# Attention issued one group less ahead of the feed-forward, its output transposed by DMA from tile 3 on, and values loaded group by group

## The chip, the cores and the metric

The kernel runs on one core of one Trainium2 chip. The metric is device time in microseconds. A core has TensorE (PE; its weight loads are PEld), VectorE (DVE), ScalarE (ACT), GpSimd (POOL) and SyncE (SP), on whose queue (SPq) all DMA issues stand. The traces list each engine's instructions as a stream of its own, and show DVE and SP keeping to program order even where a later instruction could go.

## The reference, cut to what matters

```python
# attention: batch 8, heads 8, sequence 576, head size 64, causal window of 64
scores = np.where(mask, (q @ k.T) / 8, -1e9)       # mask: 0 <= i - j < 64
x = softmax(scores) @ v                            # then to 4608 tokens x 512
# feed-forward, width 1536
g = x @ w_gate
out = (g * sigmoid(g) * (x @ w_val)) @ w_out
```

Inputs and output are float32; the kernel computes in bfloat16 with float32 sums.

## The kernel before

The 4608 tokens are 36 groups of 128. Four groups are one token tile of 512 for the feed-forward; two groups are one k/q tile of 256. For a group, attention is `scores` (16 small matmuls, exp on ACT, a product with the mask on DVE), `products` (16 small matmuls, a reciprocal and a product on DVE that give `x_b`) and a transpose of `x_b` into `xT`, which the feed-forward reads. `step(t, m)` is one feed-forward step: 4 gate and 4 value matmuls, tanh on ACT, then two DVE instructions (`sg`, `hT`) that `finish` the step before. `project` is 12 matmuls and the output write.

```python
ps_a = ctx.enter_context(tc.tile_pool(name="ps_a", bufs=3, space=PSUM))   # attention
ps_f = ctx.enter_context(tc.tile_pool(name="ps_f", bufs=2, space=PSUM))   # gate, value: 2 each

def turn1(n, nm):               # k or q, by DMA: two transposes on SP's queue
    x_b = words.pop((nm, n))
    for i in range(2):
        ...
        sp.dma_start_transpose(out=ring[:, :, o:o + P], in_=x_b[:, i])

def turn2(n, nm, eng): ...      # k or q, on PE: eight transposes and a copy on `eng`

def turn_x(g):                  # x_b -> xT on PE: four transposes and a copy on ACT
    ...
    for p in range(4):
        nc.tensor.transpose(tp[:, p, :], x_b[:, P * p:P * p + P], identb[:])
    act.copy(xT[t][:, :, off:off + P], tp[:])

def step(t, m, c0=0, n=512):
    st = gv(t, m, c0, n)        # matmuls, tanh
    if pend: finish(pend)       # sg and hT of the step BEFORE this one
    pend = st
...
for w in range(8, NG):          # one round: three steps, one group of attention, one projection
    t, s = divmod(w, 4)
    n, odd = w // 2, w % 2
    step(t, 3 * s)
    if w + 6 < NG: scores(w + 6)
    if w + 4 < NG: turn_x(w + 4)
    ...                          # casts of k and q on POOL
    step(t, 3 * s + 1)
    if w + 5 < NG: products(w + 5, (0,))
    if w + 6 < NG: cast_v(w + 6, pool)
    step(t, 3 * s + 2)
    if w + 5 < NG: products(w + 5, (1,))
    ...                          # turn1 of k or q
    project(t - 1, s)
    ...                          # loads
```

Ahead of the loop the same pieces are written out by hand, with half-width steps (`A`, `B`) and full ones (`F`). There k and q of tiles 0 to 3 are transposed on PE, of tiles 4 and later by DMA.

The softmax here doesn't subtract the row's maximum and nothing guards it: scores larger than these inputs give would overflow.

## Time and profile before

| | before |
|---|---|
| time, median of 2 | 371.24 us |
| span of the profiled run | 370.2 us |
| PE busy | 93% |
| first two waits of PE | DVE `sg` 4.8 us, DMA `qT` 4.6 us |
| usual round of the loop | 9.01 us |

The page: busy time, then rows of tenths over 40 slices of the span.

```profile
PE 345.2 (93%) x2750; PEld 181.5 (49%) x2797; DVE 231.1 (62%) x503; ACT 154.0 (42%) x276; POOL 113.5 (31%) x159
PE   8787998989779999999999999999999999999995
PEclk9999999999899999999999999999999999999999
```

PE is nearly full from slice 13 on. The two 7s in slices 11 and 12 (about 93 to 111 us) are a dip. The waits of PE (what for; us in total, times, longest) name it:

```profile
PE g_ps L237 <- DVE sg L248: 4.8, 10, 0.8
PE s_ps L161 <- DMA qT<-q_fb: 4.6, 2, 2.6
```

The windows view (columns: stretch, its length, busy time of PE, PEld, DVE, ACT and POOL, granted PE clock, DMA share, GB/s) shows a lower granted clock in the dip too, and just behind it (0.83, 0.96 and 0.87):

```profile
90.00:100.00 10.00, 7.33 (x65) 4.16 (x65) 3.47 (x10) 2.88 (x7) 4.71 (x7) 0.83 0.90 175
100.00:110.00 10.00, 7.59 (x79) 4.06 (x79) 4.41 (x12) 4.09 (x9) 2.13 (x2) 0.96 0.81 185
110.00:120.00 10.00, 9.89 (x70) 4.77 (x71) 5.37 (x12) 3.35 (x7) 3.86 (x5) 0.87 0.97 192
```

The clock record of this trace has two stretches of 3.41 us at half clock here, from 95.56 and from 109.22 us (windows view of 95.56:98.97 and of 109.22:112.63: 0.50 each); most of the second lies in the third window.

One usual round, from the timeline (start, duration, engine, line, operation). It began at 199.92 us; these lines, a selection, run from the tanh of its first step to the first matmul of its third:

```profile
201.03 0.60 ACT L242 ACTIVATE th<-g_ps 128x512 f32<-128x512 f32 x1 [0.32 <-PE g_ps L237]
201.74 0.41 PE L161 MATMUL s_ps<-qT,kT 64*128 64x64 bf16 x16
202.09 0.40 PE L205 MATMUL xtp<-identb,x_b 128*128 128x128 bf16 x4
202.19 1.08 ACT L167 ACTIVATE E<-s_ps 128x512 bf16<-128x512 f32 x2 [0.55 <-PE s_ps L161]
202.81 0.91 DVE L168 TENSOR_TENSOR E<-E,mask 128x512 bf16<-128x512 bf16 x2 [2.84 <-ACT E L167]
203.65 0.68 DVE L248 SCALAR_TENSOR_TENSOR sg<-th,g_ps 128x512 f32<-128x512 f32 x1
204.38 1.02 PE L237 MATMUL g_ps<-xT,wg 128*128 128x512 bf16 x4
```

The third step reuses the gate's PSUM buffer of the first, and `sg` is what frees it. Note also why `sg` comes so late: this `sg` belongs to the first step, and its inputs were ready when `th` ended at 201.63. DVE then stood idle until 202.81 (2.84 us in all), because the mask products of the scores come before `sg` in its program order.

### The profile page before, as it was taken

The page shows a single profiled execution, that of the slowest core. Times are in us where ns is not written, and L with a number is a line of the kernel's source. Part 1 is how long each engine was busy: PE and PEld are TensorE (multiplying, and loading weights), DVE is VectorE, ACT ScalarE, POOL GpSimd, SP SyncE. Part 2 cuts the span into 40 slices and gives each one's busy share as a digit, 9 for nine tenths or more (in the row PEclk, how much of TensorE's full clock was granted, in tenths as well). Part 3 has the DMA queues.
Part 4 walks back from the last instruction along what each step waited for, and adds up shares of the span by engine and source line. Part 5 has one row for each costly group of instructions (what it writes and reads, how often), then busy time and mean ns, then how long its engine had stood idle before and what let it go on. Part 6 is the DMA issues. An engine that isn't in the chain of part 4 may idle for free.

```text
span 370.2 us, 7165 instructions
## 1 busy us (share of the span) xinstructions
PE 345.2 (93%) x2750; PEld 181.5 (49%) x2797; DVE 231.1 (62%) x503; ACT 154.0 (42%) x276; POOL 113.5 (31%) x159
## 2 busy tenths in 40 slices
PE   8787998989779999999999999999999999999995
PEld 3456556546334444444444545444444445444442
DVE  5577798697245666666666666666666666644520
ACT  3554755444243443444344444444444443323311
POOL 2554585463314350605060606060605120000000
PEclk9999999999899999999999999999999999999999
DMA  8999999899889965857688869675744300001112
GB/s 204 322 252 266 290 313 241 150 159 188 176 186 186 197 149 119 175 124 158 132 172 120 177 123 149 147 168 126 143 96 104 87 28 30 28 30 41 44 58 85
DMA packets 147841, 54.99 MB, mean 149 GB/s; under 512 B 127328, under 2 KB 141664, under 8 KB 147808
## 3 DMA queue, kind: packets, MB, share of 16 engines
q1 hardware_dynamic: 147808, 54.54, 66.6%
q8 instruction: 22, 0.36, 0.5%
q14 instruction: 11, 0.09, 0.1%
HBM read 37.75 MB, written 9.44 MB: 127 GB/s over the span
## 4 chain that ended last, share of the span: by engine, by line
PE 74%; DVE 6%; DMA 6%; SPq 5%; ACT 5%; issue 2%; POOL 2%; ACTq 0%; POOLq 0%
PE o_ps L254 24%; PE g_ps L237 21%; PE v_ps L237 19%; DMA q_f<-in_q_dram 4%; SPq L93 4%; DVE E L168 3%; PE s_ps L161 3%; PE w_ps L266 2%; ACT E L167 2%; PE xtp L205 2%; PE ao_ps L183 2%; PE ao_ps L187 2%; DMA qT<-q_fb 1%; DVE sg L248 1%; SPq L123 1%
## 5 line engine op out<-in xcount | busy, mean ns | idle before, releaser
L237 PE MATMUL g_ps<-xT,wg 128*128 128x512 bf16 (+1 forms) x457 | 111.9, 358 | 6.9 <-DVE sg L248 4.8
L237 PE MATMUL v_ps<-xT,wv 128*128 128x512 bf16 (+1 forms) x472 | 112.3, 360 | 0.9 <-ACT wv L103 0.5
L254 PE MATMUL o_ps<-wo,hT 128*128 128x512 bf16 x419 | 98.4, 384 | 0.7
L242 ACT ACTIVATE th<-g_ps 128x512 f32<-128x512 f32 (+1 forms) x120 | 67.3, 561 | 71.0 <-PE g_ps L237 66.9
L248 DVE SCALAR_TENSOR_TENSOR sg<-th,g_ps 128x512 f32<-128x512 f32 (+1 forms) x120 | 75.1, 626 | 20.9 <-ACT th L242 20.9
L168 DVE TENSOR_TENSOR E<-E,mask 128x512 bf16<-128x512 bf16 x72 | 36.9, 526 | 74.8 <-ACT E L167 73.4
L249 DVE TENSOR_TENSOR hT<-sg,v_ps 128x512 bf16<-128x512 f32 (+1 forms) x120 | 76.1, 634 | 8.4
L237 PEld LDWEIGHTS <-wv 128*128 128x128 bf16 x480 | 47.0, 98 | 48.3 <-issue 1.4
L237 PEld LDWEIGHTS <-wg 128*128 128x128 bf16 x480 | 44.8, 98 | 41.7 <-issue 7.0
L254 PEld LDWEIGHTS <-hT 128*128 128x128 bf16 x432 | 40.8, 99 | 46.1 <-issue 2.2
L105 POOL CAST q_fb<-q_f 128x1024 bf16<-128x1024 f32 x17 | 17.9, 1053 | 114.6 <-DMA q_f<-in_q_dram 112.4
L167 ACT ACTIVATE E<-s_ps 128x512 bf16<-128x512 f32 x72 | 39.1, 596 | 20.1 <-PE s_ps L161 20.1
L105 POOL CAST ve<-v_f 64x512 bf16<-64x512 f32 x71 | 44.3, 624 | 4.4
L192 DVE TENSOR_TENSOR x_b<-ao_ps,r 128x256 bf16<-128x256 f32 x72 | 30.5, 424 | 2.5
L105 POOL CAST vo<-v_f 128x512 bf16<-128x512 f32 x36 | 22.3, 621 | 25.8 <-DMA v_f<-in_v_dram 14.2
L105 POOL CAST k_fb<-k_f 128x1024 bf16<-128x1024 f32 x17 | 18.1, 1063 | 38.1 <-DMA k_f<-in_k_dram 32.6
L183 PE MATMUL ao_ps<-ve,E 128*128 128x65 bf16 x288 | 26.6, 194 | 2.2 <-DVE x_b L192 1.2
L183 PEld LDWEIGHTS <-E 128*128 128x128 bf16 x288 | 22.0, 98 | 9.6 <-DVE E L168 1.5
L187 PE MATMUL ao_ps<-vo,E 128*128 128x65 bf16 x288 | 26.6, 194 | 0.0
L206 ACT COPY xT<-xtp 128x512 bf16<-128x512 bf16 x36 | 21.2, 590 | 12.1 <-PE xtp L205 12.1
L187 PEld LDWEIGHTS <-E 128*128 128x128 bf16 x288 | 20.1, 98 | 6.5 <-issue 0.3
L161 PE MATMUL s_ps<-qT,kT 64*128 64x64 bf16 x576 | 14.9, 191 | 7.3 <-DMA qT<-q_fb 4.6
(73 smaller groups left out, 136.3 us busy)
## 6 DMA issues: line engine op xcount, KB each, us to landing
v_f<-in_v_dram SPq DMA_DIRECT2D x32, 256.0 KB, 4.8
k_f<-in_k_dram SPq DMA_DIRECT2D x25, 256.0 KB, 3.9
q_f<-in_q_dram SPq DMA_DIRECT2D x25, 256.0 KB, 4.2
w_f<-in_moe_w_gate_dram SPq DMA_DIRECT2D x6, 512.0 KB, 7.6
w_f<-in_moe_w_val_dram SPq DMA_DIRECT2D x6, 512.0 KB, 6.5
wo_f<-in_moe_w_out_dram SPq DMA_DIRECT2D x6, 512.0 KB, 6.5
k_f<-in_k_dram SPq DMA_DIRECT2D x3, 512.0 KB, 6.9
q_f<-in_q_dram SPq DMA_DIRECT2D x3, 512.0 KB, 8.1
```

Of the source, the lines that this page charges most:

```text
L105: eng.tensor_copy(y, x)
L161: nc.tensor.matmul(ps[a][:, p, 1 - b], kT[g // 2 % KR][y, p, o:o + P], qT[g // 2 % QR][y, p, o:o + 64], tile_position=(64 * a, 0),)
L167: act.activation(e, ps[a][:], AF.Exp, scale=0.125)
L168: dve.tensor_mul(e, e, mk[:].unsqueeze(1).to_broadcast([P, 4, 2, 64]))
L183: nc.tensor.matmul(o_ps[:, i, :], E[:, e + P:e + 2 * P], ve[g % VR][:, y, :], start=True, stop=False,)
L187: nc.tensor.matmul(o_ps[:, i, :], E[:, e:e + P], vo[g % VR][:, y, :], start=False, stop=True,)
L192: dve.tensor_mul(x_b[:, 256 * h:256 * h + 256].rearrange("r (y d) -> r y d", y=4), o_ps[:, :, 0:D], r[:].unsqueeze(2).to_broadcast([P, 4, D]),
L237: nc.tensor.matmul(ps[:, 0:n], w[:, c, P * m:P * m + P], xT[t][:, c, c0:c0 + n], start=(c == 0), stop=(c == 3),)
L242: act.activation(th[:, 0:n], g_ps[:, 0:n], AF.Tanh, scale=0.5)
L248: dve.scalar_tensor_tensor(sg[:, 0:n], th[:, 0:n], 1.0, g_ps[:, 0:n], ALU.add, ALU.mult)
L249: dve.tensor_mul(hT[t][:, m, c0:c0 + n], sg[:, 0:n], v_ps[:, 0:n])
L254: nc.tensor.matmul(o_ps[:], hT[t][:, c, P * s:P * s + P], wo[:, c, :], start=(c == 0), stop=(c == 11),)
```

## The change

Its intent is to take work off PE (transposes by DMA), to ask for k, q and v later (a shorter lead), and to spread the loads. The core of the diff:

```diff
+    def load_vg(g): ...            # values of one group, not of two
+    def turn_x1(g):                # x_b -> xT by DMA
+        t, off = g // 4, P * (g % 4)
+        if off == 0:
+            xT[t] = xpool.tile([P, 4, 512], BF16, name="xT", tag="xT")
+        sp.dma_start_transpose(out=xT[t][:, :, off:off + P], in_=xb.pop(g)[:])
 # ahead of the loop: tiles 4 and 5 of k and q, and the order of all pieces (cut)
-    load1(4, k, "k_f")
-    load1(4, q, "q_f")
+    load(4, k, "k_f")              # 512-byte runs
+    load(4, q, "q_f")
-    turn1(4, "k_f")
-    turn1(4, "q_f")
+    turn2(4, "k_f", dve)           # on PE; tile 5 likewise
+    turn2(4, "q_f", act)
-    products(12)                   # and scores(13), cast_v(13), cast and turn of tiles 7 q, 8 k
     ...
     for w in range(8, NG):
         step(t, 3 * s)
-        if w + 6 < NG:
-            scores(w + 6)
         if w + 4 < NG:
-            turn_x(w + 4)
+            products(w + 4)
         ...
         step(t, 3 * s + 1)
         if w + 5 < NG:
-            products(w + 5, (0,))
+            scores(w + 5)
+        if w + 4 < NG:
+            turn_x1(w + 4)
         step(t, 3 * s + 2)
-        if w + 5 < NG:
-            products(w + 5, (1,))
         ...
         project(t - 1, s)
         ...
-        if odd and n + 4 < NB:
-            load_v(n + 4)
+        if w + 7 < NG:
+            load_vg(w + 7)
```

More of the change, by code (lines that the diff above doesn't have):

```diff
@@ L97, in load_v, with load_vg @@
         load1(n, v, "v_f")
+    def load_vg(g):
+        if g % 2 == 0:
+            staged["v_f", g // 2] = stage.tile([P, 2, H, D], FP32, name="v_f", tag="v_f")[:]
+        x_f = staged["v_f", g // 2]
+        for r, m, b, s, t in segments(P * g, P, 1):
+            sp.dma_start(x_f[r:r + m, g % 2], v[b, :, s:s + t, :].rearrange("h r d -> r h d"))
     words = {}
@@ L413 @@
     turn_x(5)
-    load1(4, k, "k_f")
-    load1(4, q, "q_f")
+    load(4, k, "k_f")
+    load(4, q, "q_f")
     load_v(4)
+    cast_k(3, "k_f", pool)
     F(0, 10)
-    cast_k(3, "k_f", pool)
     cast_k(3, "q_f", pool)
+    keys_before(3)
+    turn2(3, "k_f", dve)
+    F(0, 11)
+    turn2(3, "q_f", act)
     cast_v(6, pool)
     cast_v(7, pool)
-    F(0, 11)
-    keys_before(3)
-    turn2(3, "k_f", dve)
     A(1, 0)
-    turn2(3, "q_f", act)
+    for s in range(2):
+        casts_o(s, pool)
     A(1, 1)
-    for s in range(3):
-        casts_o(s, pool)
-    A(1, 2)
-    scores(6)
-    A(1, 3)
-    scores(7)
-    products(6)
-    for s in range(3, 6):
-        casts_o(s, pool)
-    A(1, 4)
-    turn_x(6)
-    products(7)
+    scores(6)
+    A(1, 2)
+    scores(7)
+    A(1, 3)
+    products(6)
+    A(1, 4)
+    products(7)
+    turn_x(6)
+    for s in range(2, 4):
+        casts_o(s, pool)
     A(1, 5)
@@ L443 @@
     cast_k(4, "q_f", pool)
-    turn1(4, "k_f")
-    turn1(4, "q_f")
-    keys_before(4)
-    load1(5, k, "k_f")
-    load1(5, q, "q_f")
-    load_v(5)
-    B(1, 0)
-    F(1, 6)
+    load(5, k, "k_f")
+    load(5, q, "q_f")
+    load_v(5)
+    A(1, 6)
+    B(1, 0)
+    for s in range(4, 6):
+        casts_o(s, pool)
+    B(1, 1)
+    F(1, 7)
+    keys_before(4)
+    turn2(4, "k_f", dve)
     cast_v(8, pool)
     cast_v(9, pool)
-    F(1, 7)
+    F(1, 8)
+    turn2(4, "q_f", act)
+    F(1, 9)
     scores(8)
-    F(1, 8)
+    project(0, 0)
+    B(1, 2)
+    scores(9)
     products(8)
-    F(1, 9)
-    turn_x(8)
-    scores(9)
     cast_k(5, "k_f", pool)
     cast_k(5, "q_f", pool)
-    turn1(5, "k_f")
-    turn1(5, "q_f")
-    keys_before(5)
     load1(6, k, "k_f")
@@ L469 @@
     F(1, 10)
+    turn_x(8)
     products(9)
@@ L474 @@
     turn_x(9)
-    scores(10)
-    project(0, 0)
-    B(1, 1)
-    products(10)
-    B(1, 2)
+    keys_before(5)
+    turn2(5, "k_f", dve)
+    project(0, 1)
+    B(1, 3)
+    turn2(5, "q_f", act)
     cast_k(6, "k_f", pool)
+    turn1(6, "k_f")
+    keys_before(6)
     cast_k(6, "q_f", pool)
-    turn1(6, "k_f")
     turn1(6, "q_f")
-    keys_before(6)
     load1(7, k, "k_f")
     load1(7, q, "q_f")
-    load_v(7)
+    load_vg(14)
+    B(1, 4)
+    scores(10)
+    project(0, 2)
+    products(10)
+    B(1, 5)
+    scores(11)
     turn_x(10)
-    scores(11)
-    project(0, 1)
-    B(1, 3)
+    B(1, 6)
     products(11)
     cast_v(12, pool)
-    B(1, 4)
-    turn_x(11)
-    scores(12)
-    project(0, 2)
-    B(1, 5)
-    products(12)
-    cast_v(13, pool)
     cast_k(7, "k_f", pool)
@@ L503 @@
     keys_before(7)
-    cast_k(7, "q_f", pool)
-    turn1(7, "q_f")
+    scores(12)
     load1(8, k, "k_f")
-    load1(8, q, "q_f")
-    scores(13)
     project(0, 3)
-    cast_k(8, "k_f", pool)
-    turn1(8, "k_f")
-    keys_before(8)
-    load1(9, k, "k_f")
+    turn_x(11)
     for w in range(8, NG):
@@ L519 @@
         step(t, 3 * s)
-        if w + 6 < NG:
-            scores(w + 6)
         if w + 4 < NG:
-            turn_x(w + 4)
-        if odd and n + 5 < NB:
-            cast_k(n + 5, "k_f", pool)
-        if not odd and n + 4 < NB:
-            cast_k(n + 4, "q_f", pool)
+            products(w + 4)
+        if odd and n + 4 < NB:
+            cast_k(n + 4, "k_f", pool)
+        if not odd and n + 3 < NB:
+            cast_k(n + 3, "q_f", pool)
+        if w + 5 < NG:
+            cast_v(w + 5, pool)
         step(t, 3 * s + 1)
         if w + 5 < NG:
-            products(w + 5, (0,))
-        if w + 6 < NG:
-            cast_v(w + 6, pool)
+            scores(w + 5)
+        if w + 4 < NG:
+            turn_x1(w + 4)
         step(t, 3 * s + 2)
-        if w + 5 < NG:
-            products(w + 5, (1,))
-        if odd and n + 5 < NB:
-            turn1(n + 5, "k_f")
-            keys_before(n + 5)
-        if not odd and n + 4 < NB:
-            turn1(n + 4, "q_f")
+        if odd and n + 4 < NB:
+            turn1(n + 4, "k_f")
+            keys_before(n + 4)
+        if not odd and n + 3 < NB:
+            turn1(n + 3, "q_f")
         project(t - 1, s)
         if odd and n + 5 < NB:
-            load1(n + 5, q, "q_f")
-        if odd and n + 4 < NB:
-            load_v(n + 4)
-        if not odd and n + 6 < NB:
-            load1(n + 6, k, "k_f")
+            load1(n + 5, k, "k_f")
+        if w + 7 < NG:
+            load_vg(w + 7)
+        if not odd and n + 4 < NB:
+            load1(n + 4, q, "q_f")
     flush()
```

## The prediction

> **What bounds the kernel now.** TensorE. The page gives PE 345.2 of 370.2 us (93%), and the chain of waits lies on PE for 74%. In the steady loop (w = 8 to 35, from 117 us on) the windows view shows PE busy 9.3 to 9.95 of every 10 us; one round w takes 9.02 us (timeline: rounds start at 199.92, 208.93, 217.96 us). The other loss is early: the windows 90-100 and 100-110 us have PE busy 7.3 and 7.6. The waits view names it: scores wait twice for the DMA transposes of q (4.6 us in total, 2.56 us at 92 us and 2.00 us at 106 us) (1.25 us to issue, 2.5 to 3.5 us to land, in one in-order SP queue). After each of the two waits the granted clock falls (0.83 and 0.87 in those windows): the 12 matmuls of the projection at 95.1 us take 4.29 us instead of 2.60, and about the same 1.7 us is lost from 108.8 us on. [...] So each wait costs about 4 us, the two about 8 us.
>
> **Removed.** 24 of 36 PE transposes of the attention output (groups 12 to 35), each 0.24 us of PE stream (201.74 scores, 202.08 transposes, 202.32 next step): 5.7 us, all on the critical engine. DMA transposes of k and q of tiles 4 and 5 (8 issues) leave the early queue, and their loads get 512-byte runs; so the early waits for DMA should go: up to 8 us.
>
> **Added.** 32 PE transposes (k, q of tiles 4, 5): 8 take 0.44 us, so 1.8 us, plus copies of 1.0 to 1.2 us on DVE and ACT. In the loop one DMA transpose per round: SP issue grows from about 5.5 to 6.8 us per 8.8 us round; DMA share from about 0.77 to an estimated 0.87 (512 more packets beside some 4,200).
>
> **Moved.** Attention runs one group less ahead. Values loaded per group even the queue out (3 loads each round, not 4 and 2).
>
> **New risk.** The last transpose of a token tile must land before the next tile's first step. By my reading x_b is ready about 4 us into the round, behind this round's three loads; issue 1.2 us, landing 3.5 to 5 us after issue start: 7.5 to 9 us, with the deadline near 8.7. Six such hand-overs (tiles 3 to 8) at 0 to 1 us each: I allow 1.5 us. q's lead falls to one round, about 2.5 us of slack. The early half-width steps are DVE-bound as before (0.83 us DVE against 0.87 PE, plus attention work); I allow 1.5 us for new early waits.
>
> **Sum.** 371.2 - 8.0 - 5.7 + 1.8 + 1.5 + 1.5 = 362.3. I predict 362 us, 80% range 357 to 368. Faster by over 2% (under 363.8): 0.65; within 2%: 0.31; slower: 0.04.
>
> **Would show it right.** Round period near 8.78 us; no wait of scores for qT by DMA, and granted clock 1.0 from 85 to 125 us; 48 transposes of x_b on PE; the loop starts near 110 us, not 117; DMA share in the loop up by about 0.1.
>
> **Would show it wrong.** First-step matmuls waiting for xT by DMA over 1 us per tile, with the clock falling after them; scores waiting for qT in odd rounds; load landing times growing past 6 us; new PE waits for DVE or POOL between 55 and 110 us.

The sum is 362.3 us, and its 8.0 us are the two waits (2.56 and 2.00 us) and about 1.7 us of slower matmuls behind each (4.29 us for 2.60 behind the first).

## The result

| | before | after |
|---|---|---|
| time, median of 2 | 371.24 us | 356.16 us |
| span of the profiled run | 370.2 us | 354.1 us |
| usual round | 9.01 us | 8.70 us |

The ratio is 0.9594 (95% interval 0.9553 to 0.9635). A ratio here and below is the mean time of one kernel's fast runs over that of the other's of the same rounds, so not quite the ratio of the medians quoted. The change is faster by about 15 us; 9 were predicted, and the time is 0.8 us under the predicted range.

The page after:

```profile
PE 335.0 (95%) x2696; PEld 175.6 (50%) x2741; DVE 233.4 (66%) x507; ACT 144.0 (41%) x255; POOL 113.1 (32%) x159
PE   7697999999889999999999999999999999999995
PEclk9999999999999999999999999999999999999999
```

The waits of PE, its first and the largest of scores for `qT`. No wait for a DMA of `qT` is left; that one is for a PE transpose's copy:

```profile
PE g_ps L252 <- DVE sg L263: 2.1, 4, 0.8
PE s_ps L169 <- ACT qT L111: 0.9, 2, 0.7
```

The same two windows; the clock is whole:

```profile
90.00:100.00 10.00, 8.09 (x105) 5.19 (x104) 6.24 (x19) 4.93 (x10) 1.27 (x2) 1.00 1.10 158
100.00:110.00 10.00, 9.83 (x73) 4.79 (x74) 5.82 (x12) 3.60 (x8) 5.74 (x8) 1.00 0.98 174
```

A usual round, begun at 187.11 us, from its scores to the first matmul of the next round:

```profile
191.15 0.41 PE L169 MATMUL s_ps<-qT,kT 64*128 64x64 bf16 x16
191.59 1.08 ACT L175 ACTIVATE E<-s_ps 128x512 bf16<-128x512 f32 x2 [0.55 <-PE s_ps L169]
192.22 0.91 DVE L176 TENSOR_TENSOR E<-E,mask 128x512 bf16<-128x512 bf16 x2 [0.43 <-ACT E L175]
193.05 0.68 DVE L263 SCALAR_TENSOR_TENSOR sg<-th,g_ps 128x512 f32<-128x512 f32 x1
195.81 1.03 PE L252 MATMUL g_ps<-xT,wg 128*128 128x512 bf16 x4
```

The same chain now ends at 193.73, and the step that reuses its buffer starts at 195.81, after the projection: 2.1 us of slack where there was none.

Where the 16.1 us between the two spans came from, from the starts of the rounds in the two timelines (a round runs from the first matmul of its first step to that of the next round's):

| stretch | before, us | after, us | gain, us |
|---|---|---|---|
| start to round 8 | 104.35 | 100.11 | 4.2 |
| round 8 | 12.66 | 8.70 | 4.0 |
| rounds 9 to 31 | 207.92 | 199.90 | 8.0 |
| rounds 32 to 35 and end | 45.27 | 45.39 | -0.1 |

Before, rounds 9 to 29 were mostly 9.01 us, with some of 9.13 to 9.69; after, 8.70 with one of 8.87. Rounds 30 and 31 took 0.55 us more in all than before, since a group's scores and products moved from ahead of the loop to its end.

### The profile page after: what moved, and what is told of

Read it like the earlier page. It is cut to its first block, busy times and chain, and to the rows that moved or that the text cites. A ratio compares the mean times of both kernels' runs of the same rounds, so it can differ in the third digit from the quotient of the medians.

```text
span 354.1 us, 7135 instructions
## 1 busy us (share of the span) xinstructions
PE 335.0 (95%) x2696; PEld 175.6 (50%) x2741; DVE 233.4 (66%) x507; ACT 144.0 (41%) x255; POOL 113.1 (32%) x159
## 4 chain that ended last, share of the span: by engine, by line
PE 67%; DVE 3%; issue 1%; ACT 0%; ACTq 0%
PE o_ps L269 23%; PE g_ps L252 20%; PE v_ps L252 19%; PE s_ps L169 2%; PE ao_ps L191 2%; PE ao_ps L195 1%; DVE x_b L200 1%; DVE sg L263 1%; DVE r L199 1%; ACT os__4978 L274 0%; ACTq L274 0%
## 5 line engine op out<-in xcount | busy, mean ns | idle before, releaser
L252 PE MATMUL v_ps<-xT,wv 128*128 128x512 bf16 (+1 forms) x471 | 110.5, 355 | 0.9 <-ACT wv L111 0.5
L269 PEld LDWEIGHTS <-hT 128*128 128x128 bf16 x432 | 42.0, 98 | 50.2
L252 PEld LDWEIGHTS <-wg 128*128 128x128 bf16 x484 | 42.8, 98 | 38.8 <-issue 4.4
L176 DVE TENSOR_TENSOR E<-E,mask 128x512 bf16<-128x512 bf16 x72 | 33.1, 465 | 22.6 <-ACT E L175 20.3
L199 DVE RECIPROCAL r<-ao_ps 128x4 f32<-128x4 f32 x72 | 12.7, 176 | 47.6 <-PE ao_ps L195 47.6
L191 PE MATMUL ao_ps<-ve,E 128*128 128x65 bf16 x288 | 23.2, 193 | 2.4 <-DVE x_b L200 1.2
L191 PEld LDWEIGHTS <-E 128*128 128x128 bf16 x288 | 20.1, 97 | 6.3 <-DVE x_b L200 1.5
L195 PE MATMUL ao_ps<-vo,E 128*128 128x65 bf16 x288 | 23.2, 193 | 0.0
L195 PEld LDWEIGHTS <-E 128*128 128x128 bf16 x288 | 19.0, 97 | 3.9 <-issue 0.4
L169 PEld LDWEIGHTS <-kT 64*128 64x128 bf16 x576 | 10.8, 95 | 15.4 <-issue 13.3
```

The lines of the kernel that those rows point to most:

```text
L169: nc.tensor.matmul(ps[a][:, p, 1 - b], kT[g // 2 % KR][y, p, o:o + P], qT[g // 2 % QR][y, p, o:o + 64], tile_position=(64 * a, 0),)
L176: dve.tensor_mul(e, e, mk[:].unsqueeze(1).to_broadcast([P, 4, 2, 64]))
L191: nc.tensor.matmul(o_ps[:, i, :], E[:, e + P:e + 2 * P], ve[g % VR][:, y, :], start=True, stop=False,)
L195: nc.tensor.matmul(o_ps[:, i, :], E[:, e:e + P], vo[g % VR][:, y, :], start=False, stop=True,)
L252: nc.tensor.matmul(ps[:, 0:n], w[:, c, P * m:P * m + P], xT[t][:, c, c0:c0 + n], start=(c == 0), stop=(c == 3),)
L269: nc.tensor.matmul(o_ps[:], hT[t][:, c, P * s:P * s + P], wo[:, c, :], start=(c == 0), stop=(c == 11),)
```

## The experiments

Twelve kernels, all correct. The first four start from the changed kernel and undo a part of it (lead_only undoes all but the shorter lead and the order), the next four add one part to the kernel before, and the last four followed from what these showed; each set of four ran on one chip, beside runs of the kernel before. Three theories were at stake. Theory Q: the early waits come from DMA transposes of tiles 4 and 5 that hold up SP's queue. Theory L: they come from the order, which asked for k and q too early. Theory C came later: a chain through ACT and DVE sets the pace of the loop in the old order.

| kernel | median, us | before beside it, us | ratio (95% interval) | usual round, us |
|---|---|---|---|---|
| lead_only | 365.06 | 372.52 | 0.9789 (0.9758 to 0.9820) | 8.92 |
| a_x_on_pe | 361.80 | 372.52 | 0.9708 (0.9688 to 0.9728) | 8.92 |
| a_kq45_dma | 359.19 | 372.52 | 0.9649 (0.9611 to 0.9688) | 8.70 |
| a_v_pairs | 356.06 | 372.52 | 0.9553 (0.9532 to 0.9574) | 8.70 |
| b_kq45_pe | 371.00 | 371.92 | 0.9971 (0.9943 to 0.9998) | 9.01 |
| b_x_dma | 372.43 | 371.92 | 1.0011 (0.9983 to 1.0039) | 9.01 |
| b_fused | 369.52 | 371.92 | 0.9920 (0.9881 to 0.9959) | 8.92 |
| b_v_groups | 371.21 | 371.92 | 0.9979 (0.9944 to 1.0015) | 9.01 |
| b_late_x_dma | 365.91 | 372.10 | 0.9846 (0.9790 to 0.9901) | 8.70 |
| a_scores_early | 383.06 | 372.10 | 1.0294 (1.0251 to 1.0338) | 9.87 |
| a_short_runs | 356.18 | 372.10 | 0.9570 (0.9521 to 0.9619) | 8.70 |
| i_mid_t5 | 355.09 | 372.10 | 0.9545 (0.9503 to 0.9586) | 8.70 |

### lead_only: the lead and the order alone

```diff
 # against the kernel after
-            turn_x1(w + 4)
+            turn_x(w + 4)
 # load_v pairs again; load1 and turn1 of tiles 4 and 5 again, placed as in the kernel before
```

> The changed kernel with the attention output transposed on TensorE again, k and q of tiles 4 and 5 loaded and transposed by DMA again, and values loaded in pairs again; what is left of the change is the shorter lead and the new order (both halves of the products together). Theory Q (my prediction: the early waits come from the DMA transposes of tiles 4 and 5 that hold up the SP queue): the two waits of scores for qT and the half clock after them stay, only fused products help, 367 to 370 us. Theory L (the order: TensorE now reaches the scores of tiles 6 and 7 later in its own stream, while the data come no sooner): the waits go with the order alone, 358 to 362 us.

Between the two: 7.5 us faster than the kernel before. The loop runs at 8.92 us without irregular rounds, and round 8's wait is gone. The first wait is still there, with the half clock behind it (mean clock of the profiled run 0.995):

```profile
PE s_ps L169 <- DMA qT<-q_fb: 2.8, 1, 2.8
```

So each theory has one of the two waits: the lead and the order remove the second, something else the first. This run doesn't part the shorter lead from the new order of the round, or from the fused products.

### a_x_on_pe: the attention output back on PE

```diff
 # against the kernel after
-            turn_x1(w + 4)
+            turn_x(w + 4)
```

> The changed kernel with only the attention output's transposes back on TensorE. If they are worth what the prediction says, 24 times 0.24 us, the time is 356.2 + 5.7 = 361.9 us, rounds of 8.94 us. If they also bring back waits of TensorE for VectorE or PSUM in the loop, 363 to 365 us. If the DMA transposes cost waits of their own, under 361 us.

As expected to a tenth: 361.8 us. In the new order the 24 groups' transposes are worth 5.6 us (361.80 less 356.16); rounds grow by 0.22 us, and no wait comes back in the loop.

### a_kq45_dma: tiles 4 and 5 by DMA again

```diff
 # against the kernel after; tile 5 likewise
-    load(4, k, "k_f")
-    load(4, q, "q_f")
+    load1(4, k, "k_f")
+    load1(4, q, "q_f")
     cast_k(4, "q_f", pool)
+    turn1(4, "k_f")
+    turn1(4, "q_f")
-    turn2(4, "k_f", dve)
-    turn2(4, "q_f", act)
```

> The changed kernel with k and q of tiles 4 and 5 loaded in 256-byte runs and transposed by DMA as before. Theory Q: waits of scores for qT by DMA and a half clock come back, 360 to 364 us. Theory L: no such wait, and 32 TensorE transposes of 1.8 us fewer: 354 to 356.5 us.

359.19 us, 3.0 over the kernel after (356.16), so theory Q holds for the first wait:

```profile
PE s_ps L169 <- DMA qT<-q_fb: 3.3, 1, 3.3
```

SP's queue shows how. In this kernel (timeline of SP) the transposes of tile 5 go out before the loads of tile 6, which follow them at 83.56 us:

```profile
77.18 2.52 SPq L131 DMA_TRANSPOSE kT<-k_fb  x2
80.24 3.28 SPq L131 DMA_TRANSPOSE qT<-q_fb  x2
83.56 1.96 SPq L93 DMA_DIRECT2D k_f<-in_k_dram  x3
```

In the kernel after, the loads of tile 6 go out at 76.99 us, right behind the output write of the first projection:

```profile
64.36 3.00 SPq L93 DMA_DIRECT2D v_f<-in_v_dram  x2
76.53 0.37 SPq L276 DMA_DIRECT2D out_dram<-os__1367  x1
76.99 1.81 SPq L93 DMA_DIRECT2D k_f<-in_k_dram  x3
```

Those 6.6 us are more than the wait. (Even after the change SP stands still from 67.4 to 76.5 us, behind an output write that is not ready: an order of its own making.)

### a_v_pairs: values two groups at a time again

```diff
 # against the kernel after
-        if w + 7 < NG:
-            load_vg(w + 7)
+        if odd and n + 4 < NB:
+            load_v(n + 4)
```

> The changed kernel with values loaded two groups at a time in odd rounds as before. If the waits of TensorE for VectorE in the loop of the kernel before (2.4 us over 23 rounds) came from POOL casts bunched in odd rounds beside VectorE's mask products, rounds of 9 us and 1 to 2.5 us come back: 357 to 359 us. Otherwise 356 us within 0.5.

356.06 us: nothing. Loading values group by group has no measurable part in the result.

### b_kq45_pe: only tiles 4 and 5 moved to PE, old order

```diff
 # against the kernel before; tile 5 likewise, turn2 behind F(1, 10) and F(1, 11)
-    load1(4, k, "k_f")
+    load(4, k, "k_f")
-    turn1(4, "k_f")
-    turn1(4, "q_f")
     F(1, 6)
+    turn2(4, "k_f", dve)
     F(1, 7)
+    turn2(4, "q_f", act)
     scores(8)
```

> The kernel before with only k and q of tiles 4 and 5 loaded in 512-byte runs and transposed on TensorE; lead and order stay. Theory Q: both waits for qT and the half clock go: 371.2 - 8 + 1.8 = 365 us. Theory L: the waits stay wholly or mostly, 369 to 373 us.

371.0 us, 0.3% faster. The first wait for `qT` and both half clocks are gone (mean clock of the profiled run 1.000), yet the time hardly moves. By the timeline PE reaches the step behind the first projection at 88.04 us instead of 83.64: the 32 transposes take 1.8 us, and new waits for their copies and for DVE come with them (1.10 us at the scores of tile 4 alone). Round 8 starts at 104.44 us, where the kernel before had 104.35: what the wait had cost was now lost ahead of it. Only round 8 itself gained (10.60 for 12.66 us), with a wait of 1.54 us left in it. The profile puts that wait down to DVE, but it is the second wait of before: the first transpose of q of tile 7 landed at 107.73 us and the scores started at 107.87, 0.14 us later, just as in the kernel before (landed 108.10, started 108.24).

### b_x_dma: only the attention output by DMA, old order

```diff
 # against the kernel before
-            turn_x(w + 4)
+            turn_x1(w + 4)
```

> The kernel before with only the attention output from tile 3 on transposed by DMA: 371.2 - 5.7 = 365.5 us if the 24 transposes count in full and nothing else moves; more if the transposes queue before those of k and q and lengthen the early waits (the second of them lies in the first round of the loop): 366 to 368 us.

372.43 us, 4.4 over the highest figure expected. All 96 transposes of these groups are off PE, and the rounds are still 9.01 us. In the loop PE now waits in most rounds (waits of PE, 117 to 330 us):

```profile
PE g_ps L244 <- DVE sg L255: 4.9, 20, 0.6
```

and the timeline of a round shows the chain of the kernel before, now with a visible wait at its end:

```profile
203.16 0.41 PE L161 MATMUL s_ps<-qT,kT 64*128 64x64 bf16 x16
203.60 1.08 ACT L167 ACTIVATE E<-s_ps 128x512 bf16<-128x512 f32 x2 [0.55 <-PE s_ps L161]
204.23 0.91 DVE L168 TENSOR_TENSOR E<-E,mask 128x512 bf16<-128x512 bf16 x2 [2.84 <-ACT E L167]
205.06 0.68 DVE L255 SCALAR_TENSOR_TENSOR sg<-th,g_ps 128x512 f32<-128x512 f32 x1
205.79 1.02 PE L244 MATMUL g_ps<-xT,wg 128*128 128x512 bf16 x4 [0.15 <-DVE sg L255]
```

From scores to third step: 203.16 to 205.79 is 2.63 us; before, 201.74 to 204.38 was 2.64 us. The chain sets this stretch, whatever PE does meanwhile. (The wait shown, 0.15 us, counts from the modelled end of pipelined matmuls. From the start of the last matmul before it to the start of this one, the extra time is 0.31 us, the whole of what the transposes had filled.)

### b_fused: both halves of the products together, old order

```diff
 # against the kernel before
-            products(w + 5, (0,))
+            products(w + 5)
-        if w + 5 < NG:
-            products(w + 5, (1,))
```

> The kernel before with both halves of the products of a group issued together in the loop. A round of the loop loses one change between attention and feed-forward matmuls: 0.07 to 0.10 us of each of 23 rounds, 1.6 to 2.4 us: 368.8 to 369.6 us. If fusing saves nothing, 371 us; if it brings new waits for VectorE, slower.

369.52 us (0.8% faster), rounds of 8.92 us, as expected in size. The reason expected was wrong, as b_late_x_dma shows below: there the products are split and the rounds are as short as with fused ones. The better reading is that 0.09 us of each 9.01 us were the chain's wait, hidden under the ends of pipelined matmuls; fusing puts the second half of the products in front of the third step and fills it. The early waits varied in this run (15.2 us in round 8 of the profiled run, which took 372.01 us and was the slowest of four).

### b_v_groups: only the values by group, old order

```diff
 # against the kernel before
-        if odd and n + 4 < NB:
-            load_v(n + 4)
+        if w + 8 < NG:
+            load_vg(w + 8)
```

> The kernel before with only the values loaded group by group in the loop. If bunched POOL casts made VectorE late in the loop, the rounds of 9.27 and 9.6 us become 9.01: 369 us. Otherwise 371 us within 0.5.

371.21 us, no change that the interval allows to be told from none; the irregular rounds (9.67, 9.29, 9.38) stay.

### b_late_x_dma: scores later, and the attention output by DMA

```diff
 # against the kernel before
         step(t, 3 * s)
-        if w + 6 < NG:
-            scores(w + 6)
         if w + 4 < NG:
-            turn_x(w + 4)
+            turn_x1(w + 4)
         ...
         step(t, 3 * s + 1)
+        if w + 6 < NG:
+            scores(w + 6)
         if w + 5 < NG:
             products(w + 5, (0,))
```

> The kernel before with the attention output transposed by DMA (as in b_x_dma, which gained nothing: rounds stayed at 9.01 us) and, besides, the scores of the loop moved from behind the first to behind the second feed-forward step of a round. Theory C: in the old order a chain from the scores over the exp, the two mask products and the gate product on VectorE to the third step's first matmul has no slack, so PE time taken out in front of it comes back as a wait; behind the second step the chain lies under the projection. Then rounds are 8.79 us (9.01 - 0.22), without the irregular rounds of 9.3 to 9.7: 364 to 367 us. Rival: the transposes by DMA pay only with the shorter lead; then rounds stay near 9.01 and the time above 369 us.

365.91 us, and the usual round is 8.70 us, the same as in the kernel after. Theory C holds, and the rival falls: this kernel has the long lead, values in pairs and split products. From round 12 on no round is longer than 8.75 us. It is still about 9.7 us over the kernel after, because the early waits remain (in round 8 as 1.19 us for `sg`, which on DVE stood behind a copy that had waited 2.76 us for the DMA transposes of k), and one of 2.08 us for `xT` at a tile's hand-over (a round of 12.61 us that also holds a 1.61 us wait for values).

### a_scores_early: scores back behind the first step, in the kernel after

```diff
 # against the kernel after
         step(t, 3 * s)
+        if w + 5 < NG:
+            scores(w + 5)
         if w + 4 < NG:
             products(w + 4)
         ...
         step(t, 3 * s + 1)
-        if w + 5 < NG:
-            scores(w + 5)
```

> The changed kernel with only the scores of the loop moved back to behind the first step of a round (before the products). Theory C: the third step waits for VectorE in each round, rounds of 8.95 to 9.3 us where 8.70 were: 361 to 368 us. Rival (order within the round is of no matter): 356 to 357 us.

383.06 us, 26.9 over the kernel after and slower than the kernel before: rounds of 9.87 us. The direction is theory C's, the size more than I expected, since the products now also stand between the scores and the third step, on PE and on DVE. Waits of PE from 40 us on:

```profile
PE g_ps L252 <- DVE sg L263: 13.2, 25, 0.8
PE ao_ps L191 <- ACT E L175: 8.0, 24, 0.3
```

The second line is new: products wait for a PSUM buffer that the exp has not yet freed. So this run doesn't measure the chain alone; it shows that in the kernel after, with the products together, the place of the scores decides 26.9 us. It doesn't show what that place was worth in the kernel before, where the products stand elsewhere; b_late_x_dma speaks to that.

### a_short_runs: tiles 4 and 5 on PE, but loaded in 256-byte runs

```diff
 # against the kernel after; tile 5 likewise. turn2b is turn2 for load1's order of rows
-    load(4, k, "k_f")
+    load1(4, k, "k_f")
-    turn2(4, "k_f", dve)
+    turn2b(4, "k_f", dve)
```

> The changed kernel with k and q of tiles 4 and 5 loaded in 256-byte runs as before, but still transposed on TensorE. If what helped there is that the DMA transposes no longer hold up the SP queue: 356.2 us within 0.7, no wait for qT. If it is the longer runs of the loads: the wait for qT at the scores of tile 6 comes back in part, 358 to 360 us.

356.18 us, as the kernel after. So what a_kq45_dma lost by is the queue and not the shorter runs of the loads; i_mid_t5 below agrees.

### i_mid_t5: an improvement

```diff
 # against the kernel after
-    project(0, 3)
-    turn_x(11)
+    project(0, 3, between=lambda: turn_x(11))    # after 6 of its 12 matmuls
     F(1, 9)
+    load1(6, k, "k_f")                           # ahead of the first output write
+    load1(6, q, "q_f")
     scores(8)
+    turn1(5, "k_f")                              # tile 5 by DMA, behind those loads
+    turn1(5, "q_f")
+    load_v(6)
     project(0, 0)
-    turn2(5, "k_f", dve)
-    turn2(5, "q_f", act)
 # and tile 5 cast before F(1, 8) and loaded with load1
```

> A trial of an improvement: the changed kernel with the last TensorE transposes before the loop (group 11) put in the middle of the projection before it, so that the first step of the loop need not wait for their copy (0.94 us), and with tile 5 transposed by DMA again, but the loads of tile 6 issued ahead of these transposes in the SP queue (0.9 us of TensorE less). If both pay: 354.3 us. If the transposes make the scores of tile 5 or 6 wait: 356 us or more.

355.09 us (354.88 to 355.41 in four runs), against 355.83 to 357.10 of a_short_runs, which equals the kernel after, on the same chip: about 0.3% faster than the kernel after, somewhat less than hoped. In the profiled run two hand-overs of `xT` lengthened their rounds (9.68 and 8.92 us for 8.70), which covers the 0.8 us that are missing. No scores waited for `qT` by DMA, although tile 5 is transposed by DMA again: behind the loads of tile 6 these transposes do no harm. The ratios' intervals overlap, as both carry the spread of the kernel before; the four runs of each do not. It is the fastest kernel.

## Why the prediction was wrong

The direction and most mechanisms were right; but the sum was too small by 5.9 us (15.1 measured, 9.2 predicted), and its two large terms, taken alone on the kernel before, gave next to nothing. Point by point:

- "What bounds the kernel now. TensorE." Right by busy time, wrong as a rule for the loop. A round of the old order took 9.01 us because the chain scores, exp, mask product, `sg`, third step had no slack; b_x_dma took PE work away and gained nothing. The prediction had all the numbers of that chain in the timeline it quoted, and read only PE's line.
- "24 of 36 PE transposes ... 5.7 us, all on the critical engine." The size is right in the new order (a_x_on_pe, 5.6 us), and false in the old one (b_x_dma, no gain: ratio 1.0011).
- "Moved. Attention runs one group less ahead." **This is the step that failed.** It stands in the sum with no term, and the scores' new place in the round, which goes with it in the diff, is not named at all. Lead and order alone (lead_only) are worth 7.5 us: rounds of 8.92 for 9.01, no irregular rounds (these cost 2.2 us over rounds 9 to 29), and no wait in round 8 (about 3.7 us). And the new place of the scores is what lets the transposes by DMA pay: b_late_x_dma has it with the long lead, and its rounds are 8.70 us. With 5.6 us (a_x_on_pe) and 3.0 us (a_kq45_dma) the 7.5 make 16.1, near the 16.4 between the kernel before and the one after, so these three parts make up nearly all of the gain. How the 7.5 us split between lead and order is not shown.
- "So the early waits for DMA should go: up to 8 us", put down to the queue. They went, and start to round 8 with round 8 gained 8.2 us net. But the queue gave only the first wait (a_kq45_dma, 3.0 us net of PE's 1.8 us); the second went with the lead and the order (lead_only). In the old order, moving tiles 4 and 5 to PE gave 0.9 us, not 6.2.
- "Added ... 1.8 us": right (8 transposes again took 0.44 us).
- The allowances, 1.5 us for hand-overs of `xT` and 1.5 us for new early waits: in the profiled run after one hand-over cost 0.17 us, while the early waits came about as allowed (0.67 us at 95.85 us, and 0.94 us for a copy of `xT` at the first step of the loop). The risk of the hand-overs was real, though: 2.08 us in b_late_x_dma, 0.98 us in i_mid_t5.
- "Would show it right": round 8.78, measured 8.70; no `qT` wait and whole clock, so measured; 48 PE transposes of `x_b`, so counted; DMA share in the loop, predicted up by 0.1, rose from 0.73 to 0.89 between 120 and 280 us. "The loop starts near 110 us, not 117" mislabels the start: 117.01 us was the start of round 9; it is now 108.81.

As a sum of what was mis-sized: the loop was given 4.2 us net and gave 8.0; the early part was given 4.7 net and gave 8.2. The irregular rounds themselves: where the two mask products took 1.52 us instead of 0.91 (at 137.93 us of the kernel before), POOL was casting values at the same time. The two took 0.77 and 0.83 us where most take 0.43, and the first (137.93 to 138.69) overlaps a cast recorded from 137.81 to 138.42. Spans on POOL are rough, and no run here separates the two: that the casts lengthened the products is not shown. What the runs do show is that spreading the values (a_v_pairs, b_v_groups) neither brings nor removes these rounds, while slack in the chain (b_late_x_dma) removes them.

The engine with the highest occupancy was PE at 93%, and taking the transposes from it changed nothing until the order did (b_x_dma, ratio 1.0011). To look for what ends the gaps on that engine would not have shown the chain before the change either, as in the usual round it ended without a recorded gap.

## What to carry to other kernels

Before crediting work taken from the busiest engine, follow each buffer that this engine reuses back through the other engines, and compare when it comes free with when it is wanted: a margin of 0.05 us (204.33 to 204.38 in the kernel before) is a second bottleneck. Place the long chain of a round in front of the stretch in which the busy engine needs nothing from it (here the projection: 2.1 us of slack where there was none). Where loads share an in-order queue with DMAs that wait for computed data, put the loads ahead (behind such DMAs they went out 6.6 us later in a_kq45_dma, which was 3.0 us slower), and test parts of a change both ways, added to the old kernel and taken from the new one, because they need not add up: here b_x_dma gave nothing and a_x_on_pe showed 5.6 us.

## What else the traces showed

- In the kernel before, waits of 2.56 and 2.00 us were each followed by 3.41 us at half clock; in the 3.41 us before each of these PE was busy for 0.79 and 1.42 us. A wait of 2.08 us in b_late_x_dma was not followed by half clock: that run also had a wait of 2.5 us, and its mean clock of 0.994 (2.2 us lost of 363.7) leaves room for one such stretch, which loses 1.7 us. So here a wait of 2.00 us was followed by half clock and one of 2.08 us was not; on what this depends is not shown.
- A 128x128 bf16 transpose on PE took 219 ns in the records (median), and what counts on a full PE is less: eight in a row took 0.44 us, four took 0.24 us.
- A 128x512 bf16 transpose by DMA (128 KB), of `xT` in the kernel after, took 1.2 us or more of SP's queue (median 1.55) and 2.4 to 6.0 us to land (median 4.1). The loads of k and q there took medians of 0.62 and 0.70 us of queue (most are of 256 KB), and those of 256 KB medians of 3.9 and 4.6 us to land.
- Four transposes that wait for computed data, ahead of loads in SP's in-order queue, made the loads of tile 6 go out 6.6 us later in a_kq45_dma than in the kernel after (83.56 for 76.99 us), worth 3.0 us net of the 1.8 us of PE work that this kernel saves.
